# Nine constant TensorE products of 512 columns against 96 of 64, at the start of an attention and gMLP kernel

## The chip, the cores and the metric

The kernel runs on one core of a Trainium2 chip. The metric is the device time of one execution in microseconds (us). TensorE (PE in the profile) multiplies matrices; DVE, ACT and POOL are the vector, scalar and general engines; SP only issues transfers. Sixteen DMA engines move data between HBM and the core's memory, and instructions as well.

## The reference

The program takes q, k and v of 4 batches, 8 heads, 768 positions and 64 values a head. It computes attention with 4 sink positions and a sliding window of 128, and then a gated block over the result.

```python
scores = scale * np.matmul(q, k.transpose(0, 1, 3, 2))
keep = is_sink | in_window                    # 4 sinks, the last 128 positions
a = np.exp(scores - max); a = a / (np.sum(a, axis=-1, keepdims=True) + 1e-09)
x = (a @ v), heads side by side               # (4, 768, 512)
h = gelu(x @ w_in)                            # 512 -> 1024
u, v = h[..., :512], h[..., 512:]
v_n = (v - mu) / np.sqrt(var + 1e-06) * g_ln
v_s = np.einsum('ts,bsd->btd', w_sg, v_n) + b_sg[None, :, None]
return x + (u * v_s) @ w_out
```

## The kernel before

The whole program is one list of steps, `STEPS`, written out by hand. Each word names a function and its arguments; a loop calls them one after the other, and each engine runs its own instructions in that order. An engine waits, by semaphores, for what an instruction reads and for the buffers that it writes. So a step that waits holds up everything behind it on its engine.

The work goes batch by batch, in several stages that overlap. For batch 0:

- `LPQ.g` and `LPK.g` (L243, on SP) load two heads of q or k at a time, as float32. `CPQ.g` and `CPK.g` cast them to bfloat16, on ACT, DVE or POOL as the last letter says (helper lines L197, L198 and L202).
- `TQ.0.g` and `TK.0.g` (L371) transpose them on TensorE, by twelve products with the identity. `EQ` and `EK` copy the result from PSUM to `qT` and `kT`.
- `QK.b.p.g` (L473, L478) makes scores in `sc`, one of two PSUM buffers; `EX` (L483) takes the exponential on ACT into `P`; `MK` (L490 on DVE, L493 and L496 on POOL) masks it.
- `LVH.b.i` (L269, on POOL) loads half of V into `v_sb`; `ZERO` (L343) has set its columns of ones before. `AV.b.p.k` (L519, L523, L526) multiplies `P` by V into `mm`, one of four PSUM buffers, and `NR` divides on DVE.
- Later stages: `XT` or `XD` transpose the result, `MV` and `MU` (L561, L602) multiply by w_in, `SP` (L622) by w_sg, `OU` (L639) by w_out, which `LWO` (L283, on POOL) loads. `ST` stores.

`LQ`, `LK` (L223), `LVH`, `LW`, `LWS` and `LWO` are issued by POOL in the order of the list, between POOL's own computing.

`HM.n` puts constant products on TensorE. It sets a count, and `fresh`, which gives out the next PSUM buffer, first writes that many products of the zero matrix `warm` into it (L188). The real work then overwrites them. Nothing reads them, and nothing but the fill of `warm` and the release of the buffer makes them wait. The list has `HM.9` before `TQ.0.0`, then `HM.3`, two `HM.2` and one `HM.4`, all for batch 0.

Of the kernel before, what the change touches and what calls it, by code (L numbers as in the profile page):

```python
# [17 lines left out]


STEPS = """  # L20
WARM LPQ.0 FILL LPK.0 LPK.1 LPQ.1 LPQ.2 LG MASK LPK.2 LPK.3 CPQ.0.A VSK LPQ.3 IDEN CPK.0.A IDEN2 MASK0 HM.9 TQ.0.0
TK.0.0 EQ.0.0.D EK.0.0.A VSO HM.3 QK.0.0.0 ZERO CPK.1.P QK.0.0.1.1 EX.0.0.0 LVH.0.0 EX.0.0.1 QK.0.0.2.1 CPQ.1.D TK.0.1
EX.0.0.2 LC CPQ.2.D LVH.0.1 TQ.0.1 MK.0.0.0.D EK.0.1.A TQ.0.2 EQ.0.1.D EQ.0.2.A HM.2 QK.0.1.0 CPK.2.A CPK.3.P
QK.0.1.1.1 EX.0.1.0 LQ.1.0 CPQ.3.D TK.0.2 EX.0.1.1 TK.0.3 EK.0.2.D LQ.1.1 TQ.0.3 EK.0.3.A GTR EQ.0.3.D LW.0 QK.0.2.0
# [51 lines left out]
def kernel(  # L76
# [14 lines left out]
    nc = tc.nc  # L91
# [39 lines left out]
    mm_ring = Ring("mm", 4, [128, 512], F32, psum)  # L131
# [24 lines left out]
    warm = sb.tile([128, 512], BF16, name="warm")  # L156
# [20 lines left out]
    def gated(b, hf):  # L177
        return gatedT[:, slots.setdefault((b, hf), len(slots) % 3)]

    pre = [0]  # L180

    def HM(n):
        pre[0] = n

    def fresh(ring, key):
        t = ring.new(key)
        for _ in range(pre[0]):
            nc.tensor.matmul(t if ring is mm_ring else t[:, 0, :], warm[:, 0:128], warm, start=True, stop=True)  # L188
        pre[0] = 0
        return t  # L190

# [100 lines left out]
    def GTR():  # L292
        nc.tensor.transpose(fresh(mm_ring, "g")[:, 0:KU], g_rows, iden32[0:KU, 0:KU])
# [64 lines left out]
    def turns(name, ring, b, g):  # L358
        t = fresh(mm_ring, (name, b, g))
        if HOW[b] == "F":  # L360
            for p in range(HP):
                nc.tensor.transpose(t[:, 128 * p:128 * (p + 1)], plain(ring, b, g)[:, 128 * p:128 * (p + 1)], iden32)
        elif HOW[b] == "D":
            for p in range(HP):
                nc.tensor.transpose(ps16((name, b, g), HP)[:, p, :], c16[name, b, g][:, 128 * p:128 * (p + 1)], iden)
        elif HOW[b] in "AGL":
            ps = ps16((name, b, g), NT)
            src = ring[b].rearrange("p (h t d) -> p h t d", h=H, t=NT)
            for t in range(NT):
                for hl in range(2):  # L370
                    nc.tensor.transpose(ps[64 * hl:64 * hl + 64, t, :], src[:, 2 * g + hl, t, :], iden)  # L371
        else:
            ps = ps16((name, b, g), 8)
            for tl in range(2):
                for p in range(HP):
                    c = d_model * (2 * g + tl) + 128 * p
                    nc.tensor.transpose(ps[:, HP * tl + p, :], ring[b][:, c:c + 128], iden)  # L377

    def single(name, t):
        ps = fresh(mm_ring, (name, t))  # L380
        for p in range(HP):
            nc.tensor.transpose(ps[:, 128 * p:128 * (p + 1)], ot[name, t][:, 128 * p:128 * (p + 1)], iden32)
# [278 lines left out]
    def ST(b, t):  # L661
        nc.sync.dma_start(out=out[b, 128 * t:128 * (t + 1), :], in_=ot[b, t])

    code = {f.__name__: f for f in (
        HM, WARM, IDEN2, LQ, LK, LV, CV, CQ, CK, GTR, GCP, LPQ, LPK, CPQ, CPK, LB, LFQ, LFK, FTQ, FTK, FEQ, FEK, LVH, LW, LWS, LWO, LC, LG, IDEN, FILL, MASK, MASK0, VSK, ZERO, VSO, VSM, TQ, TK, EQ, EK, DQ, DK,
        KS, SK, SX, QK, EX, MK, AV, NR, XT, XE, XD, MV, GV, BN, RS, NM, Z, MU, GU, WT, WE, SP, GT, GM, OU, RA, ST, OH, RH, SH)}
    holds = dict(h.split("<") for h in HOLDS.split())
    after = mybir.DependencyInfo(mybir.DependencyClass.Sync, mybir.DependencyReason.DATA)
# [42 lines left out]
```

## Time and profile before

| | us |
|---|---|
| median of 3 runs | 156.59 (156.43 to 156.64) |
| the profiled execution | 157.69 |
| its span | 156.0 (155.96) |
| TensorE busy | 146.7 (94%) |
| DVE, POOL, ACT busy | 123.4, 99.3, 99.0 |
| L188, all 20 products | 15 into `mm`, 5 into `sc`; 379 to 634 ns each |

The span is the time from the first to the last instruction of the profile; the execution's own time also holds what lies around it, 1.73 us here. TensorE's busy share counts products from their start to a modelled end, so that 94% doesn't mean that each of them runs at its best rate. The weight load that goes with each product is a row of its own (PEld). The profile prints 1549 products and 1549 weight loads.

### The profile page before, as it was taken

The page shows a single profiled execution, that of the slowest core. Times are in us where ns is not written, and L with a number is a line of the kernel's source. Part 1 is how long each engine was busy: PE and PEld are TensorE (multiplying, and loading weights), DVE is VectorE, ACT ScalarE, POOL GpSimd, SP SyncE. Part 2 cuts the span into 40 slices and gives each one's busy share as a digit, 9 for nine tenths or more (in the row PEclk, how much of TensorE's full clock was granted, in tenths as well). Part 3 has the DMA queues.
Part 4 walks back from the last instruction along what each step waited for, and adds up shares of the span by engine and source line. Part 5 has one row for each costly group of instructions (what it writes and reads, how often), then busy time and mean ns, then how long its engine had stood idle before and what let it go on. Part 6 is the DMA issues. An engine that isn't in the chain of part 4 may idle for free.

```text
span 156.0 us, 3856 instructions
## 1 busy us (share of the span) xinstructions
PE 146.7 (94%) x1549; PEld 94.2 (60%) x1549; DVE 123.4 (79%) x295; ACT 99.0 (64%) x110; POOL 99.3 (64%) x127
## 2 busy tenths in 40 slices
PE   6988989999999979989999999999999999999990
PEld 2445577779675756747566764486567644776530
DVE  4557789829989969969789887899789956867981
ACT  3699798799899846276897855269954025591000
POOL 4099779388999899997549869640798610300400
PEclk9999999999999999999999999999999999999999
DMA  4999999999999999999999199995710580510064
GB/s 156 282 365 151 153 197 189 166 192 193 146 143 142 193 152 139 167 156 156 168 230 246 22 285 174 178 197 60 236 71 3 102 235 0 202 63 11 0 227 179
DMA packets 86170, 24.67 MB, mean 158 GB/s; under 512 B 78660, under 2 KB 83016, under 8 KB 86152
## 3 DMA queue, kind: packets, MB, share of 16 engines
q0 software_dynamic: 64608, 11.01, 94.9%
q1 hardware_dynamic: 21544, 13.41, 33.1%
q8 instruction: 12, 0.20, 0.5%
q14 instruction: 6, 0.05, 0.1%
HBM read 24.81 MB, written 6.29 MB: 199 GB/s over the span
## 4 chain that ended last, share of the span: by engine, by line
PE 73%; DMA 17%; DVE 2%; POOL 2%; issue 1%; ACT 1%; SPq 1%; ACTq 0%
PE mm L622 17%; PE mm L639 14%; PE sc L561 13%; PE sc L602 12%; DMA w_out_sb<-in_moe_w_out_dram 7%; DMA v_sb<-in_v_dram 6%; PE sc L478 4%; DMA uT<-in_k_dram 4%; PE mm L519 3%; PE mm L377 3%; PE mm L523 2%; PE mm L526 2%; PE mm L614 1%; POOL v_sb L269 1%; PE mm L545 1%
## 5 line engine op out<-in xcount | busy, mean ns | idle before, releaser
L483 ACT ACTIVATE P<-sc 128x1024 bf16<-128x1024 f32 (+1 forms) x48 | 43.4, 953 | 10.3 <-PE sc L478 10.1
L622 PE MATMUL mm<-wsgT,z 128*128 128x384 bf16 x192 | 34.1, 327 | 0.0
L622 PEld LDWEIGHTS <-z 128*128 128x128 bf16 x192 | 17.7, 98 | 11.9 <-issue 0.7
L639 PE MATMUL mm<-w_out_sb,wsg_gated 128*128 128x512 bf16 x96 | 22.7, 379 | 1.1 <-DMA w_out_sb<-in_moe_w_out_dram 1.1
L561 PE MATMUL sc<-w_in_sb,xT 128*128 128x512 bf16 x96 | 22.2, 379 | 0.7 <-ACT vt L565 0.7
L627 DVE SCALAR_TENSOR_TENSOR gtmp<-mm,g_sb,b_bc 128x384 bf16<-128x384 f32 x32 | 19.1, 611 | 4.2 <-PE mm L622 3.6
L602 PE MATMUL sc<-xT,w_in_sb 128*128 128x256 bf16 x192 | 22.1, 273 | 0.0
L493 POOL TENSOR_SCALAR_AFFINE_SELECT P<-P 128x512 bf16<-128x512 bf16 x21 | 14.0, 667 | 12.3 <-ACT P L483 12.0
L632 POOL TENSOR_TENSOR wsg_gated<-gtmp,uT 128x384 bf16<-128x384 bf16 x15 | 14.5, 982 | 10.9 <-DVE gtmp L627 10.9
L574 DVE BATCH_NORM_STATS2 st<-vt 128x6 f32<-128x512 f32 x24 | 15.4, 685 | 7.5 <-ACT vt L565 7.4
L602 PEld LDWEIGHTS <-w_in_sb 128*128 128x128 bf16 x192 | 18.7, 98 | 3.0
L536 DVE TENSOR_TENSOR x_sb<-mm,rcp 128x384 bf16<-128x384 f32 (+1 forms) x36 | 18.5, 513 | 1.2
L643 DVE TENSOR_TENSOR ot<-mm,x_sb 128x512 f32<-128x512 f32 x24 | 16.1, 684 | 2.7 <-PE mm L639 2.5
L565 ACT ACTIVATE vt<-sc 128x1024 f32<-128x1024 f32 x12 | 12.3, 1027 | 9.0 <-PE sc L561 8.9
L583 POOL TENSOR_TENSOR rs<-rs,neg_half 128x4 f32<-128x4 f32 (+1 forms) x8 | 6.9, 867 | 17.4 <-DVE rs L578 16.0
L223 POOL DMA_DIRECT2D k<-in_k_dram x18 | 16.4, 928 | 0.7 <-DMA v_sb<-in_v_dram 0.7
L223 POOL DMA_DIRECT2D q<-in_q_dram x18 | 16.7, 952 | 0.0
L519 PE MATMUL mm<-v_sb,P 128*128 128x65 bf16 x192 | 15.9, 194 | 0.7 <-DMA v_sb<-in_v_dram 0.6
L519 PEld LDWEIGHTS <-P 128*128 128x128 bf16 x192 | 14.5, 98 | 2.8 <-issue 0.6
L639 PEld LDWEIGHTS <-wsg_gated 128*128 128x128 bf16 x96 | 9.2, 98 | 11.4 <-DMA w_out_sb<-in_moe_w_out_dram 1.4
L561 PEld LDWEIGHTS <-xT 128*128 128x128 bf16 x96 | 9.2, 98 | 10.9 <-issue 0.9
L478 PE MATMUL sc<-qT,kT 64*128 64x128 bf16 (+1 forms) x256 | 14.8, 238 | 0.6 <-DVE qT L198 0.3
(90 smaller groups left out, 244.4 us busy)
## 6 DMA issues: line engine op xcount, KB each, us to landing
out_dram<-ot SPq DMA_DIRECT2D x24, 256.0 KB, 2.3
v_sb<-in_v_dram POOLq DMA_DIRECT2D x8, 384.0 KB, 8.3
q<-in_q_dram POOLq DMA_DIRECT2D x18, 128.0 KB, 6.7
k<-in_k_dram POOLq DMA_DIRECT2D x18, 128.0 KB, 6.9
wsg_gated<-in_moe_w_sg_dram POOLq DMA_DIRECT2D x2, 576.0 KB, 8.3
w_in_sb<-in_moe_w_in_dram POOLq DMA_DIRECT2D x2, 512.0 KB, 10.2
uT<-in_q_dram SPq DMA_DIRECT2D x2, 384.0 KB, 3.2
uT<-in_k_dram SPq DMA_DIRECT2D x2, 384.0 KB
```

The lines of the kernel that those rows point to most:

```text
L223: return nc.gpsimd.dma_start(out=dst.rearrange("p (h d) -> p h d", h=H), in_=heads(src, b, i))
L478: nc.tensor.matmul(sc[:, hl, c:c + 128 * ni], at(kT, b)[rows, j, p, :], at(qT, b)[rows, i:i + ni, p, :], start=not biased, stop=(not biase ...
L483: nc.scalar.activation(out=P.new((b, p, g))[:, :, 0:w], in_=sc_ring[b, p, g][:, :, 0:w], func=AF.Exp, scale=scale)
L519: nc.tensor.matmul(av[:, il, hl, :], pt[:, hl, c:c + 128], vb[:, h, i, :], start=first, stop=False)
L536: nc.vector.tensor_mul(x_sb.get(b)[:, i0:i0 + n, 128 * p:128 * (p + 1)].rearrange("p t (h d) -> p t h d", h=2), av[:, :, :, 0:Dh], rcp[:, ...
L561: nc.tensor.matmul(hp[:, jl, :], xT[b][:, 2 * g + jl, c, :], w_in_sb[:, c, d_half:2 * d_half], start=(c == 0), stop=(c == KD - 1))
L574: nc.vector.bn_stats(out=sts[jl], in_=vt[b, g][:, jl, :])
L602: nc.tensor.matmul(hp[:, dc // 2, 256 * (dc % 2):256 * (dc % 2 + 1)], w_in_sb[:, c, 128 * dc:128 * (dc + 1)], xT[b][:, 2 * g:2 * g + 2, c, :],
L622: nc.tensor.matmul(ps[:, 0:NH], z[b][:, si, 128 * dc:128 * (dc + 1)], wsgT[:, si, NH * hf:NH * (hf + 1)], start=(si == 0), stop=(si == NT ...
L627: nc.vector.scalar_tensor_tensor(out=gtmp.new((b, hf, dc)), in0=mm_ring["g", b, hf, dc][:, 0:NH], scalar=g_sb[:, dc:dc + 1], in1=b_bc[:, N ...
L639: nc.tensor.matmul(ps, gated(b, hf)[:, dc, 128 * tl:128 * (tl + 1)], w_out_sb[:, dc, :], start=(dc == 0), stop=(dc == KU - 1))
L643: nc.vector.tensor_add(ot.new((b, t)), mm_ring["o", b, t], x_sb[b][:, t, :])
```

## The change

`HM.9` before `TQ.0.0` becomes `HS.96`. `HS` is `HM` with a second number, the columns of a product: 64 instead of 512. The other `HM` steps keep 512 columns. So nine products of 512 columns (4608 in all) are replaced by 96 of 64 (6144), each with its own weight load of the same 128 columns of `warm`, into the same PSUM buffer.

```diff
-... CPK.0.A IDEN2 MASK0 HM.9 TQ.0.0
+... CPK.0.A IDEN2 MASK0 HS.96 TQ.0.0
...
-    pre = [0]
+    pre = [0, 512]
 
     def HM(n):
-        pre[0] = n
+        pre[:] = n, 512
+
+    def HS(n):
+        pre[:] = n, 64
 
     def fresh(ring, key):
         t = ring.new(key)
         for _ in range(pre[0]):
-            nc.tensor.matmul(t if ring is mm_ring else t[:, 0, :], warm[:, 0:128], warm, start=True, stop=True)
+            nc.tensor.matmul((t if ring is mm_ring else t[:, 0, :])[:, 0:pre[1]], warm[:, 0:128], warm[:, 0:pre[1]],
+                             start=True, stop=True)
         pre[0] = 0
         return t
```

## The prediction

> **What bounds the kernel now.** I read the page's chain first, then the chain in order of time, the timeline of the first 18 us, the waits of the first 25 us, and last the DMA queues.
>
> ```profile
> PE 73%; DMA 17%; DVE 2%; POOL 2%; issue 1%; ACT 1%; SPq 1%; ACTq 0%
> ```
>
> The end is set by TensorE (PE), with DMA second. In order of time (start, length):
>
> ```profile
> 1.81 6.04 DMA uT<-in_k_dram
> ...
> 7.93 0.83 POOL k L202
> 8.76 1.76 POOL v_sb L269
> 10.52 10.03 DMA v_sb<-in_v_dram
> ...
> 20.59 0.27 PE mm L519 x3
> ```
>
> Up to 20.59 us the chain has no TensorE work: a load of K, its cast CPK.1.P on POOL, the issue of V behind it in POOL's order, the landing of V. Then it is TensorE, with one more landing in the middle (w_out, issued by POOL after a wait for TensorE):
>
> ```profile
> 44.16 0.46 PE mm L377 x8
> ...
> 44.65 0.78 POOL q L223
> ...
> 45.52 10.79 DMA w_out_sb<-in_moe_w_out_dram
> ...
> 56.35 1.04 PE mm L639 x4
> ```
>
> The changed products are at the very start, in the timeline:
>
> ```profile
> 1.25 4.02 PE L188 MATMUL mm<-warm 128*128 128x512 bf16 x9 [1.25 <-DVE warm L304]
> ...
> 4.04 0.83 ACT L197 CAST q<-uT 128x768 bf16<-128x768 f32 x1 [1.97 <-DMA uT<-in_q_dram]
> ...
> 5.20 0.76 PE L371 MATMUL mm<-iden,q 128*64 128x128 bf16 x12
> 5.87 0.53 PE L371 MATMUL mm<-iden,k 128*64 128x128 bf16 x12
> ```
>
> q is cast at 4.87, but TQ.0.0 starts at 5.20: the nine products already hold it by 0.3 us. The waits of the first 25 us (total, times, longest) show that the loads set the pace there, on DVE and on TensorE:
>
> ```profile
> DVE q L198 <- DMA z<-in_q_dram: 1.5, 2, 1.0
> ...
> DVE q L198 <- DMA uT<-in_q_dram: 1.2, 1, 1.2
> ...
> PE mm L519 <- DMA v_sb<-in_v_dram: 0.6, 2, 0.4
> ```
>
> **Part 1: the products themselves.** Removed: nine products whose weight loads stand 0.427 us apart in the timeline (2.08, 2.50, 2.93), so 1.25 + 9 x 0.427 = 5.09. Added: 96 of 64 columns. No row has 64 columns at the slow clock of the start, so bounds: at full clock the nearest row is the 65-column product of AV, with a weight load each, started at 18.80, 18.83, 18.86, so 0.030 us; at the slow clock an eighth of 0.427, 0.053 us. 96 of them end at 1.25 + 2.9 = 4.1 or 1.25 + 5.1 = 6.4. The transposes of TQ.0.0 start a pair every 0.106 us until 5.63 and every 0.056 us from 5.95 on, so the clock rises near 5.73. Taking that moment as unchanged, 84 products run slowly and 12 fast (0.36 us): end 6.09, and with the 0.11 us that lay between the last product and TQ.0.0, TQ.0.0 starts at 6.2, **1.0 us later** (bounds -0.3 and +1.3).
>
> A rule speaks for worse: the Trainium skill, "TensorE: Matmul & The Clock Gate", section Part 1, says that with hardware decode off the sequencer spends about 62 ns on each product. By that the 96 would take 5.95 us and TQ.0.0 would be 2.1 us late. The 0.030 us rows disagree (57 products start within 2.0 us at 120 us), so it moves only the last rival's chance.
>
> Who waits for TQ.0.0: at full clock it takes 0.53 as TK.0.0's row does, so it ends at 6.7 (before 5.96). EQ.0.0.D ends at 7.7 instead of 6.96, EK.0.0.A at 7.9 instead of 7.27, and QK.0.0.0 starts 0.6 us late (7.32 before). Behind EQ on DVE are VSO, ZERO and CPQ.1.D. ZERO ends at 8.4 (7.66), and CPQ.1.D waits for its load until 8.89 anyway. The first issue of V on POOL (8.71) waits for a semaphore of DVE; ZERO's first fill of v_sb ends 7.33 now, 8.1 then: 0.6 us in hand. On ACT the three exponentials and EK.0.1.A end 0.6 late, at 11.85; QK.0.1.0 waits until 12.26 for EQ.0.1.D, whose inputs are set by DMA. HM.3 and the weight loads are hidden in the same waits. EX.0.3.0 on ACT (18.65) starts after a product, with 0.9 us idle before. So part 1 costs **0**; its cover is the waits for DMA quoted above. Without that cover it would be 0.6 less the 0.21 and 0.44 us that TensorE idles before V at 17.67 and 20.59: still 0.
>
> **Part 2: the instructions.** 87 more products, each with a weight load, are 174 more instructions of TensorE. They too come by DMA. The page lists 12 packets of queue q8, 0.20 MB in all (16 KB each), for 3098 products and loads: one for about every 256. The first falls here (13.5 to 15.5 us):
>
> ```profile
> q0 software_dynamic: 2094, 0.27, 231.2%
> q8 instruction: 1, 0.02, 3.9%
> ```
>
> Its record starts at 13.80, when 120 products had run (240 instructions), and takes 1.255 us; the twelve take 0.88 to 1.28. What that does is in the landings, one for each of the 16 DMA engines. V's first half lands at 15.02 to 16.38 on fifteen and at 17.62 on the last, its second half at 18.05 to 19.32 and at 20.55: one engine is 1.24 us behind the next, the packet's own time. In the changed kernel instruction 240 is 24 products behind the constant ones, the end of TK.0.0: the fetch moves from 13.8 to **about 7 to 8 us**. There SP's loads fill the engines (97% busy from 6 to 9 us), and five are still to land, their last sixteenths at 8.87 (q.1), 9.93 (q.2), 10.98 (k.2), 12.00 (k.3) and 13.19 (q.3). Bounds for each: 0, if the packet goes to an engine that is well ahead, and +1.25. I take **+1.1**, since the engine that was last with V is one of the two that are also last with these loads (their tails are 0.6 to 0.9 us behind the others).
>
> Where that goes: CPQ.1.D, CPQ.2.D and CPQ.3.D start as their loads land, without slack. EQ.0.1.D moves from 11.26 to 12.4, QK.0.1.0 from 12.26 to 13.4, the casts and exponentials behind them alike, and HM.4, the last work before AV.0.0.0, ends near 18.5 instead of 17.4. AV.0.0.0 starts at 18.55 (17.67: 0.21 of idle time is used up), AV.0.2.0 at 21.05 (20.59: another 0.44). V itself lands as before, since its slowest engine has the same packets to move by then. That leaves **+0.45 us** on TensorE, which has next to no idle time from there to 44.6, where POOL waits for it before it issues LQ.2.2 and LWO. So w_out comes later too: bounds 0 (it lands at 56.31 whatever happens, and 1.15 us of idle time before L639 swallows the delay) and +0.45. I take **+0.4**, by the chain's own step from PE to POOL. The later fetches also move up by 174 instructions, where the chain is TensorE.
>
> The Trainium skill, "Runtime: NRT & Kernel Launch", section Instruction fetch mechanics, has the blocks of 256 instructions too, but calls crossing one mostly hidden; by that the sum would be 0, the time 156.6, which is the first rival below. V's late sixteenth disagrees.
>
> Sum: the profiled execution took 157.69 us, 155.96 of span and 1.73 around it. 155.96 + 0 + 0.4 = 156.4, or 158.1 with what lies around. The median of the plain runs, 156.59, is 1.10 below the profiled one; with the same difference added I forecast **157.0 us**.
>
> **The rivals.**
> - Hidden (0.30): the fetch meets an engine that is ahead, or w_out's idle 1.15 us takes up what is left. For it: two waits for DMA lie on the way. Against it: LWO is issued behind TensorE. Time 156.6.
> - Faster (0.22): the fetch leaves V's window and hurts nothing earlier. V then lands with its second-latest sixteenth, 19.32, and TensorE starts AV.0.2.0 when it is ready, 0.44 earlier: 156.15. The fetch at 54.28 moves as well, to about 46; w_out's last sixteenth lands at 56.31, the next at 54.71, and 1.15 us of waiting would go: 155.4 at best. It decides once the packet's engine has 1.2 us to spare when it is fetched. Against it: an engine that is always busy lands V and w_out no sooner for doing its fetch earlier. I put it at 156.1.
> - Much slower (0.08): the weight loads don't hide behind products this short at the slow clock. L188's load lasts 0.152 us there; with two in flight a product starts every 0.076 us, and if that also keeps the clock from rising, the 96 end at 1.25 + 7.3 = 8.5. TQ.0.0 is then 3.4 us late, ZERO's first fill ends near 10.5, and the issue of V moves there from 8.71. It decides once TQ.0.0 is 0.6 us later than I take it. The 1.8 us are on the chain: 158.4. Against it: AV's rows hide their loads at full clock. The 62 ns that the Trainium skill states would be a milder form of it.
>
> **Chances.** The forecast has 0.40. About 0.2%, or 0.3 us, is what a measurement here can tell from no change. Slower is 0.40 + 0.08 = 0.48, the same 0.30, faster 0.22. The range runs from 155.9, which takes in the likelier half of "faster", to 157.5, the forecast with its whole 0.45 and as much again for the packet at its longest; it leaves out "much slower" and the far end of "faster".
>
> **What would show it.** Right: 96 starts of L188 0.053 us apart, then 0.030; TQ.0.0 near 6.2; a q8 packet between 7 and 8.5 us; the casts of q later than 8.89, 9.95 and 13.21 by about 1; AV.0.2.0 near 21. Wrong: those casts in place, V landing before 20, or L639 starting its first product before 56.

## The result, and the profile after

The changed kernel is **slower**: median 157.83 us (156.80 to 158.78, 20 runs) against 156.62 (156.06 to 157.62, 20 runs) of the kernel before on the same chip; ratio **1.0066 [1.0048, 1.0085]**. Slower was the forecast, but by 0.4 us; it is 1.0 by the ratio and 1.2 by the medians, and the median lies above the range.

The two profiled executions hide this: the changed kernel's took 157.65 us with a span of 155.94, the one of before 157.69 with 155.96. The run of before that was profiled lies 1.1 us above its kernel's median. So I compared each kernel with several traces, not this pair alone.

The changed kernel's page, its chain by engine and its packets of instructions:

```profile
PE 65%; DMA 12%; POOL 8%; DVE 5%; issue 3%; ACT 2%; SPq 2%; ACTq 0%; POOLq 0%
q8 instruction: 13, 0.21, 0.6%
```

There is one packet more than before; 174 instructions were added, and the packets come one for about 256. The chain has less TensorE and more POOL and DVE. Its pieces in order of time (start, length) say where; most lines have moved down by four (L639 is L643, L493 is L497):

```profile
4.88 9.07 DMA z<-in_q_dram
13.97 0.86 DVE q L202
...
41.73 1.33 POOL v_sb L273
43.08 9.17 DMA v_sb<-in_v_dram
52.29 0.50 issue
52.79 1.81 POOL k L227 x2
54.60 0.66 POOL P L497
55.26 0.59 POOL P L500
...
58.77 0.60 POOL P L500
59.42 0.20 PE mm L527
```

First, a load of q with its cast is on the chain before 15 us, in place of K and V of batch 0. Second, from 43 to 59 us the chain isn't TensorE. It is the second half of V for batch 1 (`LVH.1.1`), which lands after 9.17 us; then POOL, which stands still until it has landed, issues `LK.2.4` and `LK.2.5` and computes the eight masks of the four steps `MK.1.p.2.P`, two for each; then the products of AV that need the masks. w_out, the landing that I had read in the middle of the chain, is gone from it: L643 starts at 55.03, not 56.35. The waits of 48 to 62 us:

```profile
POOL k L227 <- DMA v_sb<-in_v_dram: 1.1, 1, 1.1
...
PE mm L527 <- POOL P L500: 0.4, 1, 0.4
```

`LK.2.4` needs nothing of V. The trace's records show why it waits all the same: POOL's transfers of this stage take eight semaphores, 111 to 118, in turn, and `LK.2.4` is the eighth transfer behind `LVH.1.1`. So it gets V's semaphore, 111, and waits on it until V has landed. It is so in every trace of this case.

This isn't new with the change. A second trace of the unchanged kernel (`e1_before_again`, below) has the same chain there:

```profile
42.19 9.02 DMA v_sb<-in_v_dram
51.25 0.50 issue
51.75 1.82 POOL k L223 x2
53.57 0.66 POOL P L493
```

In 11 of the 12 traces that keep the list's order around these masks, the span ends 103.58 to 103.75 us after V of batch 1 has landed. The exception is the trace of before that I predicted from (104.10): there the last part of w_out landed at 56.31, 1.6 us behind the next, with a packet of instructions at 54.28 beside it, so w_out came last. I read one execution's accident as the kernel's chain.

V isn't alone, though. In seven of the 11 the chain goes by V and the masks. In the other four (`e3_12x512`, `e6_18x512`, `e7_64x72`, `e10_change_256`, all below) it goes by the K that `TK.2.1` transposes (`LK.2.2`, `LK.2.3`), and TensorE doesn't wait for the masks. In three of these and in the first trace of before the span ends 98.61 to 98.65 us after `LK.2.3` has landed. So the end follows the later of two ways that run nearly level: V's landing and 103.7 us more, or this K's and 98.6.

The timeline of the start:

```profile
1.25 4.29 PE L191 MATMUL mm<-warm 128*128 128x64 bf16 x96 [1.25 <-DVE warm L308]
...
3.94 0.83 ACT L201 CAST q<-uT 128x768 bf16<-128x768 f32 x1 [1.87 <-DMA uT<-in_q_dram]
...
5.47 0.53 PE L375 MATMUL mm<-iden,q 128*64 128x128 bf16 x12
...
8.01 0.56 DVE L202 CAST q<-uT 128x768 bf16<-128x768 f32 x1 [0.31 <-DMA uT<-in_q_dram]
```

The 96 start 0.053 us apart until 4.17 and 0.029 apart from then on. `TQ.0.0` is 0.27 us later than in the trace of before, `CPQ.1.D` 0.88 us earlier.

The first packet of instructions has moved from 13.8 to 9.5 us, and the others have come forward with it: the fifth from 54.3 to 44.3, the sixth from 62.4 to 57.3. So the fifth now falls right behind the issue of V's second half. The DMA view of 44.0 to 45.5 us, of the changed kernel:

```profile
q0 software_dynamic: 1506, 0.19, 202.3%
q8 instruction: 1, 0.02, 4.0%
```

4.0% of 16 engines for 1.5 us is 0.96 us of one engine, while the transfers of q, V and w_out are under way. In the same window of before there is no such packet:

```profile
q0 software_dynamic: 1503, 0.19, 199.0%
```

V's second half lands in 16 parts: its semaphore is raised 16 times. In the changed kernel the last part comes at 52.25 and the one before it at 51.38, 0.87 us apart; in the kernel before at 51.86 and 51.77.

### The profile page after: what moved, and what is told of

Its sections match the earlier page's. It is cut to its first block, busy times and chain, and to the rows that moved or that the text cites. A ratio compares the mean times of both kernels' runs of the same rounds, so it can differ in the third digit from the quotient of the medians.

```text
span 155.9 us, 4030 instructions
## 1 busy us (share of the span) xinstructions
PE 147.1 (94%) x1636; PEld 97.1 (62%) x1636; DVE 123.1 (79%) x295; ACT 98.9 (63%) x110; POOL 99.7 (64%) x127
## 4 chain that ended last, share of the span: by engine, by line
PE 65%; DMA 12%; POOL 8%; DVE 5%; issue 3%; ACT 2%; SPq 2%; ACTq 0%; POOLq 0%
PE mm L626 15%; PE mm L643 13%; PE sc L565 12%; PE sc L606 10%; DMA v_sb<-in_v_dram 6%; DMA z<-in_q_dram 6%; PE sc L482 5%; PE mm L523 3%; PE mm L527 2%; SPq L247 2%; POOL q L227 2%; POOL k L227 2%; POOL P L497 2%; PE mm L530 2%; POOL P L500 2%
## 5 line engine op out<-in xcount | busy, mean ns | idle before, releaser
L643 PE MATMUL mm<-w_out_sb,wsg_gated 128*128 128x512 bf16 x96 | 22.7, 379 | 0.0
L497 POOL TENSOR_SCALAR_AFFINE_SELECT P<-P 128x512 bf16<-128x512 bf16 x21 | 14.0, 667 | 12.0 <-ACT P L487 11.7
L523 PE MATMUL mm<-v_sb,P 128*128 128x65 bf16 x192 | 16.2, 194 | 0.1
L527 PE MATMUL mm<-v_sb,P 128*128 128x65 bf16 x160 | 15.5, 194 | 0.4 <-POOL P L500 0.4
L643 PEld LDWEIGHTS <-wsg_gated 128*128 128x128 bf16 x96 | 9.2, 98 | 10.2 <-DMA w_out_sb<-in_moe_w_out_dram 0.2
```

The source lines that it names most:

```text
L497: nc.gpsimd.affine_select(out=p4[:, :, :, 0:128], in_=p4[:, :, :, 0:128], compare_op=ALU.is_ge, fill=0.0, base=0, pattern=[[0, 2], [0, 2], ...
L523: nc.tensor.matmul(av[:, il, hl, :], pt[:, hl, c:c + 128], vb[:, h, i, :], start=first, stop=False)
L527: nc.tensor.matmul(av[:, il, hl, :], pt[:, hl, c:c + 128], vb[:, h, i - 1, :], start=False, stop=(i < 2 and il == n - 1 and hl == 1))
L643: nc.tensor.matmul(ps, gated(b, hf)[:, dc, 128 * tl:128 * (tl + 1)], w_out_sb[:, dc, :], start=(dc == 0), stop=(dc == KU - 1))
```

## The experiments

**The theories.** *Instructions*: the 174 instructions put a packet beside V of batch 1 and V lands later; the products themselves cost nothing. *Products*: the 96 end later, and what waits for `TQ.0.0` is late. *Early loads*: my own step, the first packet delays the loads of q and k. Beside them stands the question whether V's late landing reaches the end through POOL's masks. Ratios are to the kernel before on the same chip, with 95% intervals; V's time is from the issue of `LVH.1.1` to its last part.

### The two kernels again

`e1_before_again` has no edit, `e5_after_again` is the changed kernel as it is.

> The kernel before, unchanged, once more, for a second profile of it and for what two equal kernels differ by. All theories: ratio 1.000 within 0.002. The instruction theory (the 174 added instructions move each fetch of a 16 KB block to other work) expects the first q8 packet again near 13.8 us and the others within 2 us of where they were, since the instructions are the same. Its first profile was one of the slowest executions (157.69 against a median of 156.6); whatever makes the usual one shorter must show here, and I expect it at the wait for w_out, whose last sixteenth came 1.6 us behind the next.

> The changed kernel, unchanged, once more, beside the next three. All theories: 1.005 to 1.009. In the profiles so far the end follows one landing: V's second half of batch 1 (LVH.1.1), behind which POOL issues LK.2.4 and LK.2.5 and then makes eight masks for AV.1. Between its issue and that landing the kernels with a fetch of instructions at 43 to 51 us took 9.2 us or more (the change, 96 of 48), those without it 9.0 or less. The instruction theory, in its second form, expects that again: a q8 packet near 44 us and 9.2 us or more.

Measured: 0.9981 [0.9955, 1.0007] and 1.0049 [1.0020, 1.0078]. The loss is there again, somewhat smaller. V took 9.02 and 9.13 us, with the last part 0.45 and 0.85 behind its neighbour. In these traces `CPQ.3.D` starts at 12.87 and 13.23; in the first pair it was 13.21 and 13.97.

### Columns or instructions

```diff
 # e2_96x48, from the changed kernel
-        pre[:] = n, 64
+        pre[:] = n, 48
 # e3_12x512, from the kernel before
-... HM.9 TQ.0.0
+... HM.12 TQ.0.0
```

`e2_96x48` keeps the 174 instructions and has the 4608 columns of before; `e3_12x512` has the 6144 columns of the change and 6 instructions more than before.

> 96 products of 48 columns: the same 4608 columns as nine of 512, but the 174 instructions more. Instruction theory: as slow as the change, ratio 1.005 to 1.008, with the first q8 packet at 8 to 10 us and the casts of the last loads late by 0.5 to 1 us. TensorE-time theory (the longer products hold TQ.0.0): ratio 1.000 within 0.002, since the products end near 5.1 as before.

> Twelve products of 512 columns: the same 6144 columns as the change, but 6 instructions more instead of 174. Instruction theory: ratio 1.000 within 0.002, first q8 packet near 13.8 us. TensorE-time theory: as slow as the change, 1.005 to 1.008, with TQ.0.0 0.3 to 1.3 us late by the moment at which the clock rises.

Measured: 1.0038 [1.0007, 1.0068] and 1.0038 [1.0013, 1.0063]. They don't tell the two apart by the time alone: *Instructions* had expected 1.005 to 1.008 of the first and 1.000 of the second. The traces do better. `e2_96x48` starts `TQ.0.0` at 5.20, as before, has its packet at 43.8, and V takes 9.41. `e3_12x512` has no packet there and V takes 8.31. It is late from the start: the first issue of V, `LVH.0.0`, comes at 9.20, against 8.31 in the repeat of before and 8.35 in that of the change. But in this trace it stands behind a cast of k whose load came late (8.42 against 7.52), not behind ZERO's fill, which ended at 7.71. So why twelve products cost 0.4% one trace can't say and stays open; how long V of batch 1 takes isn't the reason.

### A whole block of instructions

```diff
 # e4_137x34, from the changed kernel
-... HS.96 TQ.0.0
+... HS.137 TQ.0.0
-        pre[:] = n, 64
+        pre[:] = n, 34
```

137 products of 34 columns are 256 instructions more than before, one packet's worth. If only the place of the packets matters, they should fall where they fell before.

> 137 products of 34 columns: 4658 columns, near those of before, and 256 instructions more, one whole 16 KB block. Instruction theory in its form of position: behind the first block the fetches fall where they fell before (13.8, 23.2, 31.4, 41.6, 54.3), and the ratio is 1.000 to 1.002; in its form of number (any added fetch costs) 1.005 or more. TensorE-time theory: 1.000 within 0.002. A theory that short products themselves do harm, by their weight loads or the clock, expects more than the change, over 1.008.

Measured: 1.0022 [0.9994, 1.0051], packets at 41.2 and 53.9 (before: 41.6 and 54.3), V in 9.01 us. The packets are back in their places, but in this trace V is hardly quicker for it than in the changed kernel (9.17 and 9.13), its last part 0.58 behind. The time leans the expected way, but the interval holds both 1 and the ratio of `e5_after_again`: not decisive.

### Twice as long, a third shorter, and the place in between

```diff
 # e6_18x512 and e8_6x512, from the kernel before
-... HM.9 TQ.0.0
+... HM.18 TQ.0.0      (e6)
+... HM.6 TQ.0.0       (e8)
 # e7_64x72, from the changed kernel: 4608 columns, 110 instructions more than before
-... HS.96 TQ.0.0
+... HS.64 TQ.0.0
-        pre[:] = n, 64
+        pre[:] = n, 72
```

> Eighteen products of 512 columns: 18 instructions more, twice the columns of before. TensorE-time theory: TQ.0.0 1.9 us late or more, so QK.0.0.0 and the fill of v_sb behind it on DVE late by 1 to 2 us, the issue of V late too, ratio over 1.008. Instruction theory alone: 1.000 to 1.003.

> 64 products of 72 columns: 4608 columns as before, 110 instructions more. The fetch that is at 54 us before and at 44 with the change must come near 49 to 51. Instruction theory, second form: it meets V's second half and w_out on one engine, ratio 1.004 to 1.010. TensorE-time theory: 1.000 within 0.002.

> Six products of 512 columns, 6 instructions fewer: TensorE is free at 3.8 us, before q is cast. TensorE-time theory, if it holds both ways: 0.3 us of TQ.0.0 are gained and the ratio is 0.997 to 1.000; if the products also hold up the rise of the clock, it is over 1.000, with the clock rising after 6.3. Instruction theory: 1.000 within 0.002.

`e6_18x512`: **1.0095 [1.0060, 1.0129]**. The timeline shows what the rival of products does when it is real:

```profile
7.97 0.53 PE L375 MATMUL mm<-iden,q 128*64 128x128 bf16 x12
...
9.77 0.31 DVE L347 MEMSET v_sb<- 128x48 bf16 x2
10.18 2.02 POOL L273 DMA_DIRECT2D v_sb<-in_v_dram  x1 [0.82 <-DVE v_sb L347]
```

`TQ.0.0` is 2.8 us later than in the kernel before, and the issue of V waits for ZERO's fill, by the way that the prediction's last rival describes. V of batch 1 then takes only 8.55 us. In the changed kernel `LVH.0.0` is issued at 7.81 and 8.35 in the two traces, before it at 8.71 and 8.31: this isn't its loss.

`e7_64x72`: 0.9991 [0.9954, 1.0028], as fast as before. Here the theory of instructions missed: I had expected a loss, since 110 more instructions move the packets too. They move to 49.1 us, near the end of V's transfer, V takes 8.43 us, and its last part is 0.09 behind. Moving the packets isn't enough; it matters where they land.

`e8_6x512`: 1.0038 [1.0010, 1.0066]. *Instructions* had expected 1.000. With six products the clock rose at 10.64 us only, and the transposes ran slowly (0.85 us for 12 products, 0.53 once the clock is up):

```profile
4.65 0.85 PE L375 MATMUL mm<-iden,q 128*64 128x128 bf16 x12 [0.66 <-ACT q L201]
```

### The instructions without the change, and the change without its place

```diff
 # e9_later_174, from the kernel before: HM.9 stays, 174 instructions more by 18 us
-... HM.3 QK.0.0.0 ... HM.2 QK.0.1.0 ... HM.2 SK.0.2 ... HM.4 AV.0.0.0
+... HS.27.57 QK.0.0.0 ... HS.18.57 QK.0.1.0 ... HS.18.57 SK.0.2 ... HS.35.58 AV.0.0.0
 # e10_change_256, from the changed kernel: HS.96 stays, 256 more than before in all
-... HM.3 QK.0.0.0 ... HM.4 AV.0.0.0
+... HS.24.64 QK.0.0.0 ... HS.24.85 AV.0.0.0
```

(`HS.n.w` is n products of w columns; the columns stay nearly the same in sum.) These two tell the theories apart best: the one leaves the first nine products alone and adds the instructions, the other keeps all that the change does there and moves the packets on to their old places.

> HM.9 as before; the 174 instructions come in by the later constant products, HM.3, HM.2, HM.2 and HM.4, which are cut into 27, 18, 18 and 35 of 57 or 58 columns (the same columns, at full clock). So the first fetch stays near 13 us and all from 20 us on fall as with the change, one near 44. Instruction theory, second form (a fetch at 43 to 45 us lies in V's second half of batch 1 and holds back its landing, and with it the end): ratio 1.003 to 1.007, V's landing 9.1 us or more behind its issue. TensorE-time theory and a theory of the early loads: 1.000 to 1.002, landing 8.4 to 9.0 behind.

> The change's 96 of 64, and HM.3 and HM.4 cut into 24 of 64 and 24 of 85, so that 256 instructions are added by 18 us and the later fetches fall as before (near 41 and 54). Instruction theory, second form: 1.000 to 1.002. TensorE-time theory: as the change, 1.005 to 1.008, because its first products are the same. If both act, the half of it, 1.003.

Measured: `e9_later_174` **1.0042 [1.0016, 1.0069]**, `e10_change_256` **1.0003 [0.9975, 1.0031]**. In the first there is a packet at 45.0 (DMA view, 44.8 to 46.2 us):

```profile
q8 instruction: 1, 0.02, 5.0%
```

V takes 9.38 us, its last part 0.55 behind. This execution took 0.7 us more than its kernel's median, and V is also issued late in it, at 43.59; not all of its span can be put down to the packet. In the second the packets are at 41.1 and 54.0, V takes 8.44, its last part 0.11 behind, and POOL stands still for half as long. The landing on the chain of `e9_later_174`, and that on the chain of `e10_change_256`, which no longer goes by V:

```profile
43.59 9.38 DMA v_sb<-in_v_dram
```

```profile
46.66 9.65 DMA k<-in_k_dram
```

POOL's timeline, the changed kernel first, then `e10_change_256`:

```profile
52.79 1.81 POOL L227 DMA_DIRECT2D k<-in_k_dram  x2 [1.11 <-DMA v_sb<-in_v_dram]
54.60 0.66 POOL L497 TENSOR_SCALAR_AFFINE_SELECT P<-P 128x512 bf16<-128x512 bf16 x1
```

```profile
51.76 1.83 POOL L227 DMA_DIRECT2D k<-in_k_dram  x2 [0.57 <-DMA v_sb<-in_v_dram]
53.57 0.68 POOL L497 TENSOR_SCALAR_AFFINE_SELECT P<-P 128x512 bf16<-128x512 bf16 x1
```

So the loss comes without the change's products and goes while they stay. It hangs on where the instructions put the packet. *Early loads* falls with *Products*, since `e10_change_256` has its first packet at 9.1 us, like the change. Both kernels also cut later constant products into short ones (four steps in `e9_later_174`, two in `e10_change_256`); as one loses and the other doesn't, that is unlikely to be the cause.

### Does it reach the end through POOL's masks?

Two edits, each made in the kernel before and in the changed one. The first exchanges `LK.2.4` and `LK.2.5`, which stand behind V's wait on POOL, with `LQ.2.4` and `LQ.2.5`, which stand ahead of it. The second puts the mask ahead of that wait.

```diff
 # swap (e11 from before, e12 from the changed kernel)
-... LQ.2.4 ... LQ.2.5 ... LK.2.4 ... LK.2.5 ...
+... LK.2.4 ... LK.2.5 ... LQ.2.4 ... LQ.2.5 ...
 # mask (e15 from before, e16 from the changed kernel)
-... GT.0.1.1 EX.1.1.2 LK.2.4 ... AV.1.3.0 MK.1.0.2.P GT.0.1.3 ...
+... GT.0.1.1 EX.1.1.2 MK.1.0.2.P LK.2.4 ... AV.1.3.0 GT.0.1.3 ...
 # both (e13 from before, e14 from the changed kernel)
```

> The kernel before with LK.2.4 and LK.2.5 in the places of LQ.2.4 and LQ.2.5 in the list, and those two behind the wait for V's landing. If the end follows that landing through K (TensorE waits 0.4 to 0.6 us for K before TK.2.2 in the profiles), the ratio is 0.995 to 0.999. If it follows it through the masks alone, 1.000.

> The changed kernel with the same swap of K and Q. If the change costs its time by the late landing of V and what is queued behind it, the swap takes back half of it or more: not over 1.003 against the kernel before, and within 0.003 of the swapped kernel before. If the change costs it elsewhere, the difference to the swapped kernel before stays 0.005 to 0.007.

> The kernel before with the swap of K and Q, and one mask, MK.1.0.2.P, moved ahead of LQ.2.4, into the time in which POOL waits for V's landing. If the end follows V's landing through the masks, POOL ends its masks 1.2 us sooner, TensorE's wait of 0.3 us for them goes, and the ratio is 0.993 to 0.998. If the masks don't matter, it is as the swap alone, 0.997.

> The changed kernel with both moves. If V's late landing costs the change its time through the masks, the difference to the kernel before with both moves falls under 0.003 (0.007 with the swap alone). If the late landing costs it in another way, it stays 0.005 to 0.007.

> The kernel before with the mask alone moved, ahead of LK.2.4. Masks: 0.996 to 0.999. K (TensorE waits 0.4 to 0.6 us for LK.2.5 before TK.2.2, and K still waits for V's landing): 1.000.

> The changed kernel with the mask alone moved. Masks: within 0.003 of the kernel before with the same move. K, or both K and masks behind V's landing: 0.004 to 0.007 slower than that, since K still waits.

| edit | in the kernel before | in the changed kernel | difference |
|---|---|---|---|
| none (e1, e5) | 0.9981 [0.9955, 1.0007] | 1.0049 [1.0020, 1.0078] | 0.007 |
| swap (e11, e12) | **0.9969 [0.9943, 0.9995]** | 1.0040 [1.0010, 1.0071] | 0.007 |
| mask (e15, e16) | 1.0078 [1.0045, 1.0110] | 1.0068 [1.0034, 1.0103] | -0.001 |
| both (e13, e14) | 1.0076 [1.0044, 1.0107] | 1.0083 [1.0051, 1.0116] | 0.001 |

By the intervals, each difference is uncertain by 0.004 to 0.005.

The swap doesn't take the difference away, against what I had expected. Its chain shows why: `LQ.2.4` now stands where `LK.2.4` stood, so it is the eighth transfer behind `LVH.1.1`, gets semaphore 111 and waits for V just the same. From V's landing to the end it takes 103.4 us in both, 0.3 less than in the unswapped kernels, and V takes 8.93 and 9.74 us. `e11_before_swap` is the one version that is faster than both kernels of this case, by 0.3%.

Once two of the eight masks run ahead of the wait, the difference is no longer seen. But the kernels are slower, by 0.7 to 0.8%, where I had expected a gain from the moved mask. In `e13_before_mask_swap` the moved masks now run from 51.67 on, beside the product of DVE that they used to come after. POOL's row and DVE's of that kernel, then DVE's of `e11_before_swap`:

```profile
51.67 0.74 POOL L493 TENSOR_SCALAR_AFFINE_SELECT P<-P 128x512 bf16<-128x512 bf16 x1
```

```profile
51.58 1.64 DVE L632 TENSOR_TENSOR wsg_gated<-gtmp,uT 128x384 bf16<-128x384 bf16 x1
```

```profile
51.01 0.47 DVE L632 TENSOR_TENSOR wsg_gated<-gtmp,uT 128x384 bf16<-128x384 bf16 x1
```

The same operation takes 1.64 us instead of 0.47, DVE is on the chain of all four such kernels from 53 us on (in `e16_after_mask` to 55.7), and in `e13_before_mask_swap` DVE's first operation that writes `ot` (L643 in the lines of the kernel before) starts at 58.70 instead of 56.09. I take it that another delay covers the difference. That fits the way through V and POOL, which these four kernels no longer end by (104.05 to 106.15 us from V's landing to the end), but it is no cure, and that the masks alone carry the delay isn't shown.

### All traces together

With a packet between 43.6 and 45.0 us (seven traces: the changed kernel twice, `e2_96x48`, `e9_later_174`, e12, e14, e16) V of batch 1 takes 9.02 to 9.74 us, 9.28 on average, and its last part comes 0.75 behind its neighbour. Without it (eleven traces) it takes 8.31 to 9.19, 8.68 on average, the last part 0.27 behind. Single traces overlap (without the packet `e4_137x34` took 9.01, the repeat of before 9.02 and `e15_before_mask` 9.19); the means are 0.6 us apart. When V is issued doesn't explain it: 42.8 us on average with the packet, 43.0 without. The four comparisons of the old order with the packet there gave 1.0066, 1.0049, 1.0038 and 1.0042, 0.77 us on average. How much of it V's delay can be is bounded by the other way. In the four traces of these kernels the end comes 0.65 to 0.74 us later than the landing of `LK.2.3` and 98.6 us more, 0.70 on average; in the eight traces of the old order without the packet 0 to 0.62, about 0.20 on average. That leaves about 0.5 us for V, most of the loss, as an estimate from single traces. The rest is within the intervals, and I can't place it. Open stays as well that `e3_12x512` and `e8_6x512` lose 0.4% with no packet there.

## Why the prediction was right or wrong

- **The products end later: right in kind, smaller.** Starts 0.053 and then about 0.030 us apart held. `TQ.0.0` was 0.27 us later, not 1.0, because I took the clock's rise as fixed at 5.73, and it came at 4.20. With rises at equal times (3.89 in the repeat of before, 3.94 in that of the change) it is 4.71 against 5.35, 0.64 later. Six traces start with these 96 (the change twice, `e10_change_256`, e12, e14, e16) and five as before (before twice, e11, e13, e15): in the six `TQ.0.0` starts at 5.35 to 6.48, in the five at 4.71 to 5.20, on average 0.78 earlier. So the step was sound but for the moment of the clock's rise. The 62 ns per product that the prediction weighs beside it aren't seen.
- **Part 1 costs nothing: right where the clock rises early, with less cover than I thought.** In the two traces of the change `TQ.0.0` starts at 5.47 and 5.35, and `LVH.0.0` is no later than before; over the six it is issued at 8.57 on average, over the five at 8.83. `e6_18x512` shows the cover gone at 7.97. In `e10_change_256`, with the same 96 products, the clock rose at 6.76: `TQ.0.0` starts at 6.48, ZERO's fill ends at 8.85 and `LVH.0.0` comes behind it at 9.16. So late executions may pay some tenths here; that kernel's ratio of 1.0003 says that it isn't much on average. "Much slower" didn't happen.
- **The first packet moves to 7 to 8.5 us: nearly** (9.5, and 8.7 in the repeat; in the first trace 147 products had started by then, not 120).
- **It delays the loads of q by 1.1 us, and TensorE by 0.45: this step failed.** Two traces of the changed kernel have `CPQ.1.D` at 8.01 and 8.75, two of the kernel before at 8.89 and 8.45; `CPQ.3.D` at 13.97 and 13.23 against 13.21 and 12.87. A part may be real, but one kernel's two traces differ by as much, and over the six traces and the five `CPQ.3.D` starts at 13.62 and 13.44 on average, 0.2 later. The first product of AV starts at 17.67 in the six and 17.74 in the five, so TensorE's 0.45 didn't come. What it would do didn't arrive either: `LVH.1.1` is issued at 43.08 and 42.40 against 43.25 and 42.19. The reason that I gave for 1.1, that the engine of the packet is also last with these loads, rests on nothing that a view shows: the 16 parts of a landing come without the number of their engine.
- **"V itself lands as before": wrong.** V of batch 0 landed at 20.19 and 19.14 against 20.55 and 19.47, about 0.35 earlier (over the six traces and the five, 19.61 and 20.08 on average). The time is near that of the "faster" rival, but its reason doesn't hold: packets didn't leave this transfer. One is at 9.5 us, as V is issued, and one at 17.1, which takes 1.5 us, and in the first trace V's last part is still 1.42 us behind its neighbour. Why it lands earlier stays open.
- **"The later fetches also move up by 174 instructions, where the chain is TensorE": the failed step that matters.** It is costed at nothing and is most of the loss. One of them goes to 44.3, beside V of batch 1, where the chain isn't TensorE; V takes 9.28 us on average with a packet there and 8.68 without, and with the packet the chain goes by V in all four traces of the old order. I had found a packet's price in the landings of V of batch 0, 1.24 us, and then didn't put the moved packets beside the other transfers. V of batch 1 had landed at 51.86 on the trace of before, 0.5 us ahead of `LK.2.4`; I didn't ask what a later landing would do, since the chain showed w_out there. Yet POOL already stood still for V on that trace, in its timeline:

```profile
52.40 1.82 POOL L223 DMA_DIRECT2D k<-in_k_dram  x2 [0.72 <-DMA v_sb<-in_v_dram]
```

- **w_out.** The "faster" rival was right that the packet at 54.28 would leave it: w_out lands at 54.99 and L643 starts at 55.03. It gained nothing on the medians. The repeat of before doesn't have the wait (w_out lands at 53.86), and even where it stood it wasn't worth 1.15 us: the next work of TensorE is `TK.2.1`, whose second half needs `LK.2.3`; that landed at 57.34 on that trace, and the second half started at 57.45, so some 0.1 us was to be had.
- **Hidden (0.30): wrong, but near.** The Trainium skill, "Runtime: NRT & Kernel Launch", section Instruction fetch mechanics, has a fetch as mostly hidden. In these traces the price that could be found is paid by a transfer beside the packet, and by the times whether it is hidden goes by place: with packets at 41 and 54 us (`e10_change_256`) or at 49 (`e7_64x72`) it was, at 44 it wasn't.
- **The direction was right for another reason than mine.** The 0.4 stood for a delay of TensorE at 20 us that the traces don't show; the loss came from a landing at 52 us that I had left out. That the sign came out right is luck, and two of the prediction's own signs of being wrong showed: `CPQ.1.D` wasn't late, and L643 started before 56 us.

## What to carry to other kernels

When a change adds instructions, list each packet of instructions at its new place against every load in flight there, and cost the landing of each load that something waits for, later ones included. Read the chain from more than one execution: a landing that is last in one may not be in the next, and the one behind it sets the time. Ask of each wait for a landing whether it is for the data or for a semaphore that is used again. To separate instructions from the work they do, pad until 256 are added: where the loss goes, as in `e10_change_256`, it was the place (`e4_137x34`, padded at the start, left it undecided).

## What was unexpected of the hardware

- **The clock rises at another moment in each execution.** With nine or more long products at the start, or 64 to 137 short ones, it rose between 3.89 and 7.07 us, at 5.73 and 3.89 in two traces of the same kernel. With six products it rose at 10.64 in the one trace taken.
- **A packet of instructions beside the loads of 44 us takes 0.88 to 1.40 us of one DMA engine's time** (0.96 in the changed kernel), and V's last part of sixteen then lands 0.41 to 0.96 us behind its neighbour (0.09 to 0.58 without). Which engine it takes isn't in the views; that it is the one that lands last is inferred from the size.
- **A bf16 product on DVE takes 1.64 us instead of 0.47 with two of POOL's masks beside it** (e13 against e11; 1.64 to 1.84 in the four kernels with the moved mask). That alone is more than the change under study costs. The size isn't fixed: beside masks at 113 us the same operation takes 0.78 in e13, and 0.36 at 81 us with nothing of POOL beside it.
